# A long convolution and its expert layers: third stage one chunk later, last stage behind the first stage's visit, results stored whole

## The chip, the cores and the metric

The kernel runs on one core of one Trainium2 chip. A core has TensorE (matrix products into PSUM), VectorE (DVE), ScalarE (ACT), GpSimd (POOL) and SyncE (SP), which here issues every transfer between the chip's memory (HBM) and the core's SBUF. The engines run side by side, each through its own list of instructions in order, and wait for each other by semaphores. The metric is the time of one execution on the device in microseconds. All data are 32-bit floats.

## The reference

```python
def _attn_ref(x, v, pos_emb, w1, w2):          # x, v: (4, 12480, 128)
    h_mlp = np.maximum(pos_emb @ w1, 0.0) @ w2
    h_filt = h_mlp * np.exp(-0.01 * np.arange(S))[:, None]
    u = x * v
    Uf = np.fft.rfft(u, n=2 * S, axis=1)
    Hf = np.fft.rfft(h_filt, n=2 * S, axis=0)
    y = np.fft.irfft(Uf * Hf[None], n=2 * S, axis=1)[:, :S]
    return x * y

def _moe_ref(x, w_in, w_out):                  # x: (49920, 128), d_ff = 2048
    h = x @ w_in
    return (h * np.clip(h + 3.0, 0.0, 6.0) / 6.0) @ w_out
```

The result of the first function, reshaped to 49920 tokens, is the input of the second. So there is a causal convolution along the sequence, for every channel with its own filter, and then two dense layers with a gate between them.

## The kernel before, in words

**Convolution.** The Fourier transform along the sequence is split into products with small tables of sines and cosines. The 128 channels are taken in 4 groups of G = 32 and the 4 batches in 2 pairs, which makes NG = 8 groups of work, each with COLS = 128 columns. Two buffers z in SBUF hold the transforms of two groups at a time. For a group there are these stages:

- *First stage* (`first_stage`, L274): matmuls with `ctab` (L282) turn u = x * v into z; ScalarE copies the product from PSUM to z (L294). It is done in *visits* (`visit`, L457) of VISIT = 4 calls, for the group after the current one. The product x * v is made by GpSimd (`gate_next`, L453), which also sends for the next x and v (L442).
- *Spectra*, or second stage (`spectra`, L488; matmuls L301): K2 = 99 frequencies in NCHUNK = 25 chunks of CH = 4, each with a table `tab` of 256 KB that SP loads (`load_tab`, L471).
- *Products* (`products`, L503): ScalarE copies the spectra with their halves exchanged into the one bank `sw` (L499, L500); VectorE multiplies with the filter `h` (L520 to L523) into q, a, q2 and a2; GpSimd adds these (L527). SP loads the next `h` in two transfers of 128 KB (`load_h`, L484) into one of NH = 4 buffers.
- *Third stage* (`third_stage`, L536; matmuls L542): the same `tab` takes the sum `a` back; ScalarE copies it into z (L550). Then the table's buffer, one of NT = 7, is free and the next table is sent for.
- *Back* (`back`, L552): TensorE transposes four columns of z (L557) into a bank `ts`, and ScalarE copies them to `w` (L560). Sixteen columns fill a `w`, which is put on the list `pend`.
- *Fourth, or last, stage* (`fourth_stage`, L564): eight matmul records with `dtab` (L574) into two `ts` banks, a ScalarE copy to `o` (L584), a sum and a difference on VectorE (L586) give `y`. SP stores `y` row block by row block to the result tensors `yd`, in the order in which the expert layers will read, and the rows that fit no block of 32 to `ye` (L592, L595).

PSUM has eight banks: two for the spectra, one for `sw`, one for the third stage, and four `ts` banks that first stage, transposes and last stage share.

**The order of the work.** It is written out by hand (`manual_schedule`), and each engine does its share in that order. `period(g)` (L599) goes through the 25 chunks of a group. Chunk c does `products` of chunk c, `third_stage` of the chunk LAG - 1 = 2 before, `load_tab`, and `spectra` of chunk c + 1. Behind it come the transposes (`back`) of the group before, about 1.45 a chunk from chunk 2 on, each with up to three steps of decoding the expert weights (`weight`, L637; VectorE instructions L226 to L248, on up to group 6). After every fourth transpose comes one `fourth_stage` (from the eighth on; so it takes the `w` of one visit earlier) and then the visit of the next group. The `w` left over at the end of a group is taken in chunk 0 of the next group (L631). In group 0 nothing is transposed; in group 7 there is no visit.

**Turn-over.** `finish` (L653) does the last third stages, `last_turn` (L657) the 32 transposes and the last stages of group 7, with the first two loads of the expert layers among them.

**Expert layers** (class `Moe`, from L672): 98 tiles of 512 tokens, of which two hold the rows left over (`is_rest`). `load` (L709) brings x and the convolution's result `yt`, the latter in one transfer (L728), or for the two special tiles in transfers of one row's eighth (L722). `gate` (L733) multiplies them (L741), `turn` (L749) transposes and splits into high and low halves, `up` and `down` are the two layers, each in three matmuls per block (L768 to L770, L803 to L807), since a product is made of high and low parts. In tile t, `load(t + 2)` and `gate(t + 1)` are written out at steps 1 and 2 of 8.

Of the kernel before, what the change touches and what calls it, by code (L numbers as in the profile page):

```python
# [9 lines left out]
F32 = mybir.dt.float32  # L10
# [16 lines left out]
B, S, D = 4, 12480, 128  # L27
FO = 64
DFF = 2048
N1 = 64  # L30
N2 = 196
K2 = 99
NF = N1 * N2
R = (98, 97)
L = R[0] * N1
RH = R[0] // 2 + 1

G = 32
GB = 2
GY = 16  # L40
# [19 lines left out]

LAG = 3
NU = 2
# [3 lines left out]
GATES0 = (0, 2, 4, 8, 11, 14, 17, 20, 22)  # L66
NT = 7
NH = 4
# [91 lines left out]
def hyena_moe(ctx, tc, x, v, xt, pos_emb, w1, w2, w_in, w_out, c_tab, d_tab, f_tab, g_tab, win_d, ident_d, out):  # L160
# [4 lines left out]
    hd = [dram.tile([D // G // 2, P, K2, 2, G], F32, name=f"hd{h}") for h in range(2)]  # L165
    yd = [[dram.tile([NR, 4, 32, G // GH, N1, GH], F32, name=f"yd{b}_{k}") for k in range(2)] for b in range(B)]
    ye = dram.tile([len(REST), D // GH, N1, GH], F32, name="ye")
    wd = [dram.tile([2, P, DFF], F32, name=f"wd{i}") for i in range(2)]
# [8 lines left out]
    with tc.manual_schedule():  # L177
        conv = Conv(tc, nc, left, right, x, v, c_tab, d_tab, g_tab, ident, hd, yd, ye, weights)
        conv.filter(pos_emb, w1, w2, f_tab, win_d, ident_d)
        for g in range(NG):  # L180
            conv.period(g)
        conv.finish()
        left.close()
        moe = Moe(ctx, tc, nc, xt, wd, yd, ye, out)
        conv.last_turn(moe)
        right.close()
        moe.run()
# [64 lines left out]
class Conv:  # L252
    def __init__(self, tc, nc, left, right, x, v, c_tab, d_tab, g_tab, ident, hd, yd, ye, weights):
        self.tc, self.nc, self.left, self.right = tc, nc, left, right
        self.x, self.v, self.g_tab, self.ident, self.hd, self.yd = x, v, g_tab, ident, hd, yd
        self.c_tab, self.d_tab, self.weights, self.ye = c_tab, d_tab, weights, ye
        self.loaded, self.gated, self.n_loaded = [], [], 0
# [245 lines left out]
    def products(self, item):  # L503
# [4 lines left out]
        hs = self.hs.pop(0)  # L508
        a = self.pr.tile([P, CH, 2 * GB, G], F32, tag="a", name="pa")
        a2 = self.pr.tile([P, CH, 2 * GB, G], F32, tag="a2", name="pa2", bufs=2)  # L510
        q = self.pr.tile([P, CH, GB, G], F32, tag="q", name="pq", bufs=2)
        q2 = self.pr.tile([P, CH, GB, G], F32, tag="q2", name="pq2", bufs=2)
        uv = t.rearrange("p (k s g) -> p k s g", k=CH, g=G)[:, :kw]
# [38 lines left out]
    def back(self, g, col):  # L552

        nc = self.nc
        t = self.bank(("ts", "s2")[col // 4 % 2] if g == NG - 1 else "ts")
        for i in range(4):
            nc.tensor.transpose(t[:K2, i * 128 : (i + 1) * 128], self.z[g % 2][:, :, col + i], self.ident)  # L557
        if col % GY == 0:
            self.w = self.wp.tile([K2, GY, 128], F32, tag="w", name="w", bufs=3)
        nc.scalar.copy(self.w[:, col % GY : col % GY + 4, :].rearrange("p c m -> p (c m)"), t[:K2, :])  # L560
        if col % GY == GY - 4:
            self.pend.append((g, col + 4 - GY, self.w))

    def fourth_stage(self):  # L564
# [23 lines left out]
        k, b, d = self.place(g, piece)  # L588
        for h in range(2):
            e = ch // GH + h  # L590
            for i, p, q, r, n in PARTS:
                nc.sync.dma_start(self.yd[b][k][q, d // G, r : r + n, e], y[64 * h + p : 64 * h + p + n, i])  # L592
            for i, p, r in ((0, 49, 49), (1, 1, 97)):
                if r < R[k]:
                    nc.sync.dma_start(  # L595
                        self.ye[REST.index((b, k, r)), d // GH + e].unsqueeze(0), y[64 * h + p : 64 * h + p + 1, i]
                    )

    def period(self, g):  # L599
# [7 lines left out]
        for c in range(NCHUNK):  # L607
# [4 lines left out]
            while n < end:  # L612
# [4 lines left out]
                if n % VISIT == 0:  # L617
                    if n > VISIT:
                        self.fourth_stage()
                    if g + 1 < NG:  # L620
                        self.visit(g + 1, n // VISIT - 1)

    def chunk(self, g, c):
# [4 lines left out]
        if len(self.second) >= LAG:  # L628
            self.third_stage(self.second.pop(0))
            self.load_tab()  # L630
        if g > 1 and c == 0:  # L631
            self.fourth_stage()
        g, c = (g, c + 1) if c + 1 < NCHUNK else (g + 1, 0)
# [38 lines left out]
class Moe:  # L672
# [6 lines left out]

    def __init__(self, ctx, tc, nc, x, wd, yd, ye, out):  # L680
        self.ctx, self.tc, self.nc = ctx, tc, nc
        self.x, self.yd, self.ye, self.out = x, yd, ye, out
        P = 128
# [25 lines left out]
    def load(self, t):  # L709
# [4 lines left out]
        if self.is_rest(t):  # L714
            i = self.tiles[t]
            s = REST.index(i[0])
            for j in range(4):
                for m in range(len(i)):
                    a = self.ye[s + m, 4 * j : 4 * j + 4].rearrange("e (h r) c -> r h e c", r=32)
                    for h in range(2):  # L720
# [4 lines left out]
        else:  # L725
            b, k, q, n = self.tiles[t]
            a = self.yd[b][k][q].rearrange("q r e n c -> (q r) e n c")[:, :, n : n + self.NB, :]
            nc.sync.dma_start(  # L728
                y.rearrange("p (e m) -> p e m", e=4), a.rearrange("p e n c -> p e (n c)")
            )  # L730
        self.loaded[t] = xt, y

    def gate(self, t):  # L733
# [141 lines left out]
```

## Time and profile before

| What | Value |
|---|---|
| Median of 3 runs | 3256.47 us (3252.92 to 3272.07) |
| Profiled execution, device time | 3259.06 us |
| Its span, first to last instruction | 3257.3 us |
| TensorE, matmuls | 3156.4 us (97%) |
| ScalarE | 2356.5 us (72%) |
| VectorE | 2315.7 us (71%) |
| GpSimd | 2079.7 us (64%) |
| Bytes moved | 296.70 MB, mean 91 GB/s |

"Line engine op out<-in" names a group of instructions; "<-" behind a time names what ended the wait in front of it. PE is TensorE, PEld its weight loads, SPq the issuing of transfers on SP. A 32-bit matmul leaves two records, so eight records of L301 or L542 are the four matmuls of a chunk. The granted clock is TensorE's, as a share of full speed. The span is not the same everywhere: the filter's transform is made up to about 160 us, then come the eight groups, then a turn-over, and from about 1141 us the expert layers.

### The profile page before, as it was taken

How to read it: one execution, taken by the hardware profiler on the slowest of the kernel's cores; microseconds unless marked ns; L12 is line 12 of the kernel's file. 1: busy time of each engine (PE TensorE's matmuls, PEld its weight loads, DVE VectorE, ACT ScalarE, POOL GpSimd, SP SyncE). 2: the span in 40 equal slices, each digit the busy share in tenths (PEclk: the TensorE clock that was granted, in tenths of full speed). 3: DMA queues.
4: the chain of work that ended last, by engine and by line, in shares of the span. 5: the costliest groups of instructions: out<-in, count | busy, mean ns of one | idle time of the engine just before them, and what ended most of it. 6: DMA issues, size and time to landing. Idle time of an engine off the chain costs nothing.

```text
span 3257.3 us, 53858 instructions
## 1 busy us (share of the span) xinstructions
PE 3156.4 (97%) x20026; PEld 2667.5 (82%) x20026; DVE 2315.7 (71%) x2691; ACT 2356.5 (72%) x3039; POOL 2079.7 (64%) x1242
## 2 busy tenths in 40 slices
PE   9989899899899899999999999999999999999999
PEld 8988787787787588888888888888888888888887
DVE  4456676676656377777777777777777777777776
ACT  2356666666676577778877787778777877787777
POOL 1177767767767166666666666666666666666666
PEclk9999999999999999999999999999999999999999
DMA  6677777777765401011111111111111110111010
GB/s 232 198 202 193 206 194 196 206 200 193 203 173 168 141 30 39 30 36 39 39 39 34 36 39 39 33 36 40 39 30 39 39 39 30 39 39 39 30 39 23
DMA packets 236980, 296.70 MB, mean 91 GB/s; under 512 B 38727, under 2 KB 159854, under 8 KB 235694
## 3 DMA queue, kind: packets, MB, share of 16 engines
q1 hardware_dynamic: 236718, 293.26, 31.7%
q8 instruction: 158, 2.59, 0.3%
q14 instruction: 104, 0.85, 0.1%
HBM read 224.87 MB, written 68.29 MB: 90 GB/s over the span
## 4 chain that ended last, share of the span: by engine, by line
PE 66%; DMA 1%; SPq 0%; POOL 0%; ACT 0%; issue 0%; DVE 0%; DVEq 0%; ACTq 0%
PE acc L807 11%; PE acc L803 11%; PE acc L804 11%; PE ph L769 11%; PE ph L770 11%; PE ph L768 11%; DMA yd<-y 1%; PE ts L574 0%; PE ts L557 0%; SPq L592 0%; PE s L557 0%; DMA yt<-yd 0%; PE s L542 0%; PE s L301 0%; DMA ye<-y 0%; DMA tab<-in_g_tab 0%
## 5 line engine op out<-in xcount | busy, mean ns | idle before, releaser
L792 POOL TENSOR_TENSOR glo<-g,ghi 128x1024 fp32r<-128x1024 f32 x588 | 1404.3, 2396 | 775.4 <-ACT ghi L790 775.2
L780 DVE SCALAR_TENSOR_TENSOR g<-r,ph 128x1024 f32<-128x1024 f32 (+1 forms) x784 | 949.3, 1211 | 413.8 <-ACT r L778 413.6
L778 ACT ACTIVATE r<-ph,three 128x1024 f32<-128x1024 f32 (+1 forms) x784 | 871.4, 1112 | 277.6 <-PE ph L770 277.5
L790 ACT CAST ghi<-g 128x1024 fp32r<-128x1024 f32 (+1 forms) x784 | 811.1, 1035 | 5.4 <-DMA ye<-y 4.2
L768 PE MATMUL ph<-xhi,win_hi 128*128 128x512 f32 (+1 forms) x1568 | 609.1, 388 | 2.3 <-DVE y L586 2.3
L803 PE MATMUL acc<-ghi,wout_hi 128*128 128x512 f32 (+1 forms) x1568 | 608.6, 388 | 2.3 <-ACT ghi L790 2.3
L769 PE MATMUL ph<-xlo,win_hi 128*128 128x512 f32 (+1 forms) x1568 | 608.8, 388 | 0.0
L770 PE MATMUL ph<-xhi,win_lo 128*128 128x512 f32 (+1 forms) x1568 | 608.8, 388 | 0.0
L804 PE MATMUL acc<-ghi,wout_lo 128*128 128x512 f32 (+1 forms) x1568 | 608.6, 388 | 0.0
L807 PE MATMUL acc<-glo,wout_hi 128*128 128x512 f32 (+1 forms) x1568 | 481.8, 388 | 1.0 <-POOL glo L792 1.0
L527 POOL TENSOR_TENSOR pa<-pa,pq 128x256 f32<-128x256 f32 (+1 forms) x400 | 290.3, 732 | 247.4 <-DVE pa L521 220.8
L768 PEld LDWEIGHTS ph<-xhi,win_hi 128*128 128x128 f32 x1568 | 294.7, 188 | 64.2 <-issue 2.7
L803 PEld LDWEIGHTS acc<-ghi,wout_hi 128*128 128x128 f32 x1568 | 294.7, 188 | 63.4 <-ACT ghi L790 2.8
L807 PEld LDWEIGHTS acc<-glo,wout_hi 128*128 128x128 f32 x1568 | 294.0, 188 | 62.4 <-POOL glo L792 2.0
L770 PEld LDWEIGHTS ph<-xhi,win_lo 128*128 128x128 f32 x1568 | 294.6, 188 | 60.7
L804 PEld LDWEIGHTS acc<-ghi,wout_lo 128*128 128x128 f32 x1568 | 294.6, 188 | 60.6
L769 PEld LDWEIGHTS ph<-xlo,win_hi 128*128 128x128 f32 x1568 | 294.6, 188 | 60.5
L792 DVE TENSOR_TENSOR glo<-g,ghi 128x1024 fp32r<-128x1024 f32 x196 | 283.3, 1446 | 0.0
L520 DVE TENSOR_TENSOR pq<-s,h 128x256 f32<-128x256 f32 (+1 forms) x200 | 84.1, 420 | 280.0 <-POOL pa L527 124.3
L542 PE MATMUL s<-pa,tab 128*128 128x128 f32 x1694 | 242.3, 289 | 40.5 <-POOL pa L527 30.3
L542 PEld LDWEIGHTS s<-pa,tab 128*128 128x128 f32 x1694 | 212.4, 197 | 64.4 <-POOL pa L527 50.0
L741 DVE TENSOR_TENSOR xy<-xt,yt 128x512 f32<-128x512 f32 x96 | 260.3, 2711 | 0.0
(60 smaller groups left out, 3675.4 us busy)
## 6 DMA issues: line engine op xcount, KB each, us to landing
tab<-in_g_tab SPq DMA_DIRECT2D x192, 256.0 KB
h<-hd SPq DMA_DIRECT2D x384, 128.0 KB
xt<-in_xt SPq DMA_DIRECT2D x98, 256.0 KB
out<-o SPq DMA_DIRECT2D x97, 256.0 KB
xt<-in_x SPq DMA_DIRECT2D x64, 384.0 KB
vt<-in_v SPq DMA_DIRECT2D x64, 384.0 KB
yt<-yd SPq DMA_DIRECT2D x96, 256.0 KB
yd<-y SPq DMA_DIRECT2D x256, 64.0 KB
```

The lines of the kernel that those rows point to most:

```text
L527: nc.gpsimd.tensor_tensor(out=x, in0=x, in1=y, op=add)
L542: nc.tensor.matmul(t[:, i * 128 : (i + 1) * 128], tab[:, i, :], a[:, i].rearrange("p s g -> p (s g)"), start=(n == 0), stop=(n == len(term ...
L768: nc.tensor.matmul(ph[:, i, :ne], self.win_hi[:, sl], hi[:, :ne], start=True, stop=False)
L769: nc.tensor.matmul(ph[:, i, :ne], self.win_hi[:, sl], lo[:, :ne], start=False, stop=False)
L770: nc.tensor.matmul(ph[:, i, :ne], self.win_lo[:, sl], hi[:, :ne], start=False, stop=True)
L778: nc.scalar.activation(r[:, :, :ne], ph[:, :, :ne], AF.Relu, bias=self.three)
L780: nc.vector.scalar_tensor_tensor(out=g[:, :, :ne], in0=r[:, :, :ne], scalar=6.0, in1=ph[:, :, :ne], op0=ALU.min, op1=ALU.mult)
L790: nc.scalar.copy(ghi[:, :, :ne], g[:, :, :ne])
L792: e.tensor_tensor(out=glo[:, :, :ne], in0=g[:, :, :ne], in1=ghi[:, :, :ne].bitcast(F32), op=ALU.subtract)
L803: nc.tensor.matmul(a, self.wout_hi[:, f, :], ghi[:, i, :ne], start=(f == 0), stop=False)
L804: nc.tensor.matmul(a, self.wout_lo[:, f, :], ghi[:, i, :ne], start=False, stop=False)
L807: nc.tensor.matmul(a, self.wout_hi[:, f, :], glo[:, i, :ne], start=False, stop=(f == NFC - 1))
```

## The change

It has three parts.

1. *Lag and buffers.* LAG goes from 3 to 4, so a chunk's third stage comes three chunks behind its products and no longer two. The tables get eight buffers for seven, `a` four for three, and `a2`, `q` and `q2` three for two. `w` goes from three to two.
2. *Place of the last stage.* After every fourth transpose the visit comes first and `fourth_stage` right behind it, from the fourth transpose on, so it takes the `w` just filled. The call in chunk 0 is gone.
3. *Layout of the results.* `yd` takes the form of `y`, and one transfer of 512 KB stores a whole `y`. `ye` is gone. The expert layers' `load` now picks the rows out: one transfer for each of four channel groups where the block of 32 rows comes from one piece (two blocks of three), and two for each where it is made of 17 and 15 rows; the two special tiles take single rows from `yd` in as many transfers as before.

```diff
-LAG = 3
+LAG = 4
 NU = 2
 START = 2
 VISIT = 4
 GATES = (1, 4, 8, 11, 14, 17, 20, 22)
 GATES0 = (0, 2, 4, 8, 11, 14, 17, 20, 22)
-NT = 7
+NT = 8
 NH = 4
...
     dram = ctx.enter_context(tc.tile_pool(name="dram", bufs=1, space=DRAM))
     hd = [dram.tile([D // G // 2, P, K2, 2, G], F32, name=f"hd{h}") for h in range(2)]
-    yd = [[dram.tile([NR, 4, 32, G // GH, N1, GH], F32, name=f"yd{b}_{k}") for k in range(2)] for b in range(B)]
-    ye = dram.tile([len(REST), D // GH, N1, GH], F32, name="ye")
+    yd = [[dram.tile([D // G, G // GY, 2 * 64, 2, N1, GH], F32, name=f"yd{b}_{k}") for k in range(2)] for b in range(B)]
     wd = [dram.tile([2, P, DFF], F32, name=f"wd{i}") for i in range(2)]
     w_in = w_in.bitcast(I32).rearrange("p (q k c) -> q p k c", k=NW, c=2)
     w_out = w_out.bitcast(I32).rearrange("(q f p) (k c) -> q p f k c", f=NW // D, p=P, c=2)
...
         g, c, kw, t, tab = item
         sw = self.swapped(t, kw)
         hs = self.hs.pop(0)
-        a = self.pr.tile([P, CH, 2 * GB, G], F32, tag="a", name="pa")
-        a2 = self.pr.tile([P, CH, 2 * GB, G], F32, tag="a2", name="pa2", bufs=2)
-        q = self.pr.tile([P, CH, GB, G], F32, tag="q", name="pq", bufs=2)
-        q2 = self.pr.tile([P, CH, GB, G], F32, tag="q2", name="pq2", bufs=2)
+        a = self.pr.tile([P, CH, 2 * GB, G], F32, tag="a", name="pa", bufs=4)
+        a2 = self.pr.tile([P, CH, 2 * GB, G], F32, tag="a2", name="pa2")
+        q = self.pr.tile([P, CH, GB, G], F32, tag="q", name="pq")
+        q2 = self.pr.tile([P, CH, GB, G], F32, tag="q2", name="pq2")
         uv = t.rearrange("p (k s g) -> p k s g", k=CH, g=G)[:, :kw]
         sv = sw.rearrange("p (k s g) -> p k s g", k=CH, g=G)[:, :kw]
...
         for i in range(4):
             nc.tensor.transpose(t[:K2, i * 128 : (i + 1) * 128], self.z[g % 2][:, :, col + i], self.ident)
         if col % GY == 0:
-            self.w = self.wp.tile([K2, GY, 128], F32, tag="w", name="w", bufs=3)
+            self.w = self.wp.tile([K2, GY, 128], F32, tag="w", name="w")
         nc.scalar.copy(self.w[:, col % GY : col % GY + 4, :].rearrange("p c m -> p (c m)"), t[:K2, :])
         if col % GY == GY - 4:
             self.pend.append((g, col + 4 - GY, self.w))
...
             nc.vector.tensor_tensor(out=y[:, i], in0=same, in1=o, op=op)
         piece, ch = divmod(col, G)
         k, b, d = self.place(g, piece)
-        for h in range(2):
-            e = ch // GH + h
-            for i, p, q, r, n in PARTS:
-                nc.sync.dma_start(self.yd[b][k][q, d // G, r : r + n, e], y[64 * h + p : 64 * h + p + n, i])
-            for i, p, r in ((0, 49, 49), (1, 1, 97)):
-                if r < R[k]:
-                    nc.sync.dma_start(
-                        self.ye[REST.index((b, k, r)), d // GH + e].unsqueeze(0), y[64 * h + p : 64 * h + p + 1, i]
-                    )
+        nc.sync.dma_start(self.yd[b][k][d // G, ch // GY], y)
     def period(self, g):
...
                     self.weight(n)
                 n += 1
                 if n % VISIT == 0:
-                    if n > VISIT:
-                        self.fourth_stage()
                     if g + 1 < NG:
                         self.visit(g + 1, n // VISIT - 1)
+                    self.fourth_stage()
     def chunk(self, g, c):
...
         if len(self.second) >= LAG:
             self.third_stage(self.second.pop(0))
             self.load_tab()
-        if g > 1 and c == 0:
-            self.fourth_stage()
         g, c = (g, c + 1) if c + 1 < NCHUNK else (g + 1, 0)
         if g < NG:
             self.first.append(self.spectra(g, c))
...
         y = self.io.tile([128, 512], F32, tag="y", name="yt", bufs=3)
         nc.sync.dma_start(xt, self.x[t])
         if self.is_rest(t):
-            i = self.tiles[t]
-            s = REST.index(i[0])
-            for j in range(4):
-                for m in range(len(i)):
-                    a = self.ye[s + m, 4 * j : 4 * j + 4].rearrange("e (h r) c -> r h e c", r=32)
+            for m, (b, k, r) in enumerate(self.tiles[t]):
+                i, p = (0, r) if r < RH else (1, R[0] - r)
+                for j in range(4):
+                    a = self.parts(b, k, j, i, p, p + 1)[0].rearrange("e (h r) c -> r h e c", r=32)
                     for h in range(2):
                         cols = slice(64 * m + 32 * h, 64 * m + 32 * h + 32)
                         nc.sync.dma_start(
...
                         )
         else:
             b, k, q, n = self.tiles[t]
-            a = self.yd[b][k][q].rearrange("q r e n c -> (q r) e n c")[:, :, n : n + self.NB, :]
-            nc.sync.dma_start(
-                y.rearrange("p (e m) -> p e m", e=4), a.rearrange("p e n c -> p e (n c)")
-            )
+            for i, p, block, r, m in PARTS:
+                for j in range(4 if block == q else 0):
+                    a = self.parts(b, k, j, i, p, p + m)[:, :, n : n + self.NB, :]
+                    nc.sync.dma_start(
+                        y[32 * j + r : 32 * j + r + m, :].rearrange("r (e m) -> r e m", e=4),
+                        a.rearrange("r e n c -> r e (n c)"),
+                    )
         self.loaded[t] = xt, y
+
+    def parts(self, b, k, j, i, p0, p1):
+
+        return self.yd[b][k][j].rearrange("f (e p) i n c -> i p (f e) n c", p=64)[i, p0:p1]
     def gate(self, t):
```

The rest of the diff takes `ye` out of the lists of arguments.

More of the change, by code (lines that the diff above doesn't have):

```diff
@@ L177, in hyena_moe @@
     with tc.manual_schedule():
-        conv = Conv(tc, nc, left, right, x, v, c_tab, d_tab, g_tab, ident, hd, yd, ye, weights)
+        conv = Conv(tc, nc, left, right, x, v, c_tab, d_tab, g_tab, ident, hd, yd, weights)
         conv.filter(pos_emb, w1, w2, f_tab, win_d, ident_d)
@@ L183, in hyena_moe @@
         left.close()
-        moe = Moe(ctx, tc, nc, xt, wd, yd, ye, out)
+        moe = Moe(ctx, tc, nc, xt, wd, yd, out)
         conv.last_turn(moe)
@@ L252, with __init__ @@
 class Conv:
-    def __init__(self, tc, nc, left, right, x, v, c_tab, d_tab, g_tab, ident, hd, yd, ye, weights):
+    def __init__(self, tc, nc, left, right, x, v, c_tab, d_tab, g_tab, ident, hd, yd, weights):
         self.tc, self.nc, self.left, self.right = tc, nc, left, right
         self.x, self.v, self.g_tab, self.ident, self.hd, self.yd = x, v, g_tab, ident, hd, yd
-        self.c_tab, self.d_tab, self.weights, self.ye = c_tab, d_tab, weights, ye
+        self.c_tab, self.d_tab, self.weights = c_tab, d_tab, weights
         self.loaded, self.gated, self.n_loaded = [], [], 0
@@ L678, with __init__ @@
     NB = 16
-    def __init__(self, ctx, tc, nc, x, wd, yd, ye, out):
+    def __init__(self, ctx, tc, nc, x, wd, yd, out):
         self.ctx, self.tc, self.nc = ctx, tc, nc
-        self.x, self.yd, self.ye, self.out = x, yd, ye, out
+        self.x, self.yd, self.out = x, yd, out
         P = 128
```

## The prediction

> **What bounds the kernel now.** I read the page first, for the engine that is never free, then the same busy times by stage, with the stages cut where a group's first second-stage matmul starts.
>
> ```profile
> span 3257.3 us, 53858 instructions
> PE 3156.4 (97%) x20026; PEld 2667.5 (82%) x20026; DVE 2315.7 (71%) x2691; ACT 2356.5 (72%) x3039; POOL 2079.7 (64%) x1242
> ```
>
> In the next rows the columns are the window, its length, busy PE, PEld, DVE, ACT and POOL, the granted clock, the DMA engines' share and GB/s: group 0, groups 1 to 6, group 7, the turn-over, the expert layers.
>
> ```profile
> 160.00:252.00 92.00, 82.68 (x999) 78.38 (x1000) 47.25 (x98) 54.92 (x104) 68.73 (x68) 1.00 0.79 199
> 252.00:978.20 726.20, 662.60 (x6601) 581.58 (x6600) 478.54 (x870) 474.92 (x896) 515.21 (x496) 0.97 0.74 196
> 978.20:1064.00 85.80, 81.46 (x567) 68.80 (x566) 55.14 (x110) 59.15 (x110) 63.26 (x71) 1.00 0.57 167
> 1064.00:1141.00 77.00, 65.03 (x287) 43.43 (x287) 27.55 (x40) 38.59 (x62) 13.91 (x11) 0.91 0.44 138
> 1141.00:3257.30 2116.30, 2111.97 (x9362) 1750.13 (x9360) 1631.92 (x1362) 1677.66 (x1754) 1397.03 (x586) 1.00 0.12 36
> ```
>
> The expert layers are TensorE without a hole (2112.0 of 2116.3): nothing to win there. In groups 1 to 6 TensorE is idle for 726.2 - 662.6 = 63.6 us, and the clock 0.97 takes more. Group 0 has 9.3 us idle, group 7 4.3, the turn-over 12.0. TensorE's waits in groups 1 to 6 (total, times, longest) say where the 63.6 come from:
>
> ```profile
> PE s L542 <- POOL pa L527: 22.4, 38, 1.6
> PE s L301 <- DMA tab<-in_g_tab: 19.1, 11, 3.1
> PE ts L557 <- DVE y L586: 15.3, 5, 3.5
> PE s L301 <- DVE pa L521: 2.6, 1, 2.6
> PE s L542 <- ACT sw L499: 2.3, 1, 2.3
> ```
>
> The clock hangs on these waits: in the windows view, the 3.6 us that hold a table wait of 1.72 us run at 1.00, the next 3.4 us at 0.50, whatever is in them.
>
> ```profile
> 642.00:645.60 3.60, 1.88 (x15) 1.72 (x14) 2.26 (x6) 1.77 (x4) 3.03 (x4) 1.00 1.10 261
> 645.60:649.00 3.40, 3.40 (x17) 3.40 (x17) 3.26 (x7) 2.60 (x5) 2.37 (x3) 0.50 1.10 258
> ```
>
> A mean of 0.97 over 726.2 us is a loss of 3%, about 20 us: some twelve such stretches, each costing half of 3.4. So a floor for groups 1 to 6 is 726 - 64 - 20 = 642 us, 107 a group; with the other stages' idle time the convolution could give back about 100 us.
>
> **The stores leave SP's queue.** TensorE's timeline around that table wait, then SP's:
>
> ```profile
> 624.21 1.16 PE L542 MATMUL s<-pa,tab 128*128 128x128 f32 x8 [0.86 <-POOL pa L527]
> ...
> 641.35 1.06 PE L542 MATMUL s<-pa,tab 128*128 128x128 f32 x8
> 644.13 1.13 PE L301 MATMUL s<-z,tab 128*128 128x128 f32 x8 [1.72 <-DMA tab<-in_g_tab]
> ```
>
> ```profile
> 628.73 1.53 SPq L592 DMA_DIRECT2D yd<-y  x4
> 630.31 0.25 SPq L595 DMA_DIRECT2D ye<-y  x1
> 630.60 1.46 SPq L592 DMA_DIRECT2D yd<-y  x4
> 632.10 0.86 SPq L595 DMA_DIRECT2D ye<-y  x1
> ...
> 638.99 0.54 SPq L471 DMA_DIRECT2D tab<-in_g_tab  x1
> ```
>
> Counting loads back from the stalled L301 (seven buffers), its table went into the buffer that the L542 at 624.21 released by 625.4; SP issued the load only at 638.99, 13.6 us later, and 4.6 us ahead of need. In between, one result tile alone took 1.53 + 0.25 + 1.46 + 0.86 = 4.1 us of SP. The change puts one issue there. Not seen before; nearest is the table load's 0.54, so 3.6 us saved eight times a group, 29 us of SP's 121. Table and filter loads move forward by about a result tile's 3.6 us, more where two tiles lie ahead, against a longest wait of 3.1. Of the 19.1 us I take 15; the bounds are 19.1 and 0 (if transfers, not issuing, are late).
>
> What the store adds: SP stops on it until y is complete, and the next chunk's h and tab loads queue behind. It is issued after y in both kernels, and y comes one visit (2.9 us, below) later, less than the 3.6 saved: nothing, at worst as much as the gain. It moves the whole tile, 512 KB for about 390, so 1 MB a group more. What the DMA engines do in group 4:
>
> ```profile
> q1 hardware_dynamic: 16701, 24.22, 75.5%
> yd<-y SPq DMA_DIRECT2D x16, 34.0 KB
> ```
>
> 75.5% of 120.7 us is 91 us for 24.2 MB; 25.2 MB take 95 at that rate, still under 107.
>
> The Trainium skill, "DMA: Bandwidth & Descriptors", section "Why a DMA increments its semaphore by 16 and not by 1", lets a transfer use the largest count up to 16 that divides its outer size: the 34.0 KB stores (17 rows) would sit on one DMA engine, the new 128-row store on all. By it that engine is freed as well, and the term would be nearer 19 than 15; no view here tells the engines apart.
>
> **The last stage behind the visit.** DVE and TensorE at one of the five waits for y:
>
> ```profile
> 721.13 1.43 DVE L242 SCALAR_TENSOR_TENSOR dec<-dec 128x256 f32<-128x256 int32 x1
> 722.49 1.27 DVE L586 TENSOR_TENSOR y<-ts,o 128x512 f32<-128x512 f32 x2
> ```
>
> ```profile
> 716.40 1.94 PE L574 MATMUL ts<-w,dtab 99*64 99x512 f32 x8
> 718.17 2.91 PE L282 MATMUL ts<-ctab,u 97*64 97x99 f32 x64
> 723.82 1.14 PE L557 MATMUL ts<-ident,z 128*99 128x128 f32 x4 [2.73 <-DVE y L586]
> ```
>
> L586 stands behind weight decoding on DVE and holds a ts bank; the visit uses up the others, and the next transpose stops. Afterwards the visit runs first, decoding ends under it, and after L574 come third stage and spectra (1.06 + 1.13 us above), which need no ts bank. I take 14 of 15.3; bounds 15.3 and 0. The moved o copy and y put the next chunk's products about 1.3 us (L586) later; the third stage's extra chunk, over 2 us, covers that.
>
> L574 now reads a w just copied; the 2.91 us of L282 cover the copy. Group 7 has no visit. The nearest rows are the turn-over's last, where L574 directly follows the transposes:
>
> ```profile
> 1117.61 1.07 PE L574 MATMUL ts<-w,dtab 99*64 99x512 f32 x2 [1.82 <-ACT w L560]
> 1119.07 1.93 PE L574 MATMUL ts<-w,dtab 99*64 99x512 f32 x6 [0.39 <-ACT w L560]
> ```
>
> The upper bound is 8 x 2.2 = 18 us; ScalarE was behind with expert work there, and the first quarter of L574 needs only older columns. The lower is 0. I take the 0.39 row and half as much again, 0.6 x 8 = +5. The call at chunk 0 merely moves its 1.9 us. Two w buffers do: one filling, one waiting.
>
> **The third stage a chunk later.** GpSimd's adds in group 4 (count, busy, mean ns):
>
> ```profile
> L527 POOL TENSOR_TENSOR pa<-pa,pq 128x256 f32<-128x256 f32 x48 | 35.3, 745 | 29.2 <-DVE pa L521 27.4
> L527 POOL TENSOR_TENSOR pa<-pa,pa 128x512 f32<-128x512 f32 x24 | 30.9, 1289 | 1.9
> ```
>
> A chunk costs GpSimd 2 x 0.745 + 1.289 = 2.8 us, more than the 2.2 us a chunk without transposes costs TensorE: at a group's start TensorE catches up. Over the group GpSimd is busy 515 of 726, so one chunk of lead, at least 2.2 us, covers each single wait (longest 1.6). But the last stage no longer fills chunk 0 (1.9 us), so I take 16 of 22.4; bounds 22.4 and 0. The third product buffer lets DVE run on, and eight tables keep the prefetch as deep as seven did: with the two one-off waits (2.6 and 2.3) 4 us, bounds 5 and 0. Group 0 gives 2 of 9.3, group 7 3 of 4.3.
>
> The lag has a price. A group's last chunk, 24, now goes through the third stage in chunk 2 of the next group, right ahead of that group's first transpose, which reads all of z; before, a whole chunk lay between. ScalarE's copy to z stands behind the next chunk's two sw copies. The nearest rows are the turn-over's first transpose, directly behind its z copy, and one sw copy's group:
>
> ```profile
> 1074.69 1.18 PE L557 MATMUL ts<-ident,z 128*99 128x128 f32 x4 [0.57 <-ACT z L550]
> ```
>
> ```profile
> L500 ACT ACTIVATE sw<-s 64x512 f32<-64x512 f32 (+1 forms) x200 | 113.1, 566 | 6.4
> ```
>
> So a new wait of 0.57 us with ScalarE free, 0.57 + 2 x 0.57 = 1.7 with both copies ahead, in seven groups: 4 to 12 us. I take 8; the lower end is 0, if the spectra between cover it.
>
> **The clock.** Where the waits go, so do the half-speed stretches: 16 of 20 us, as the GpSimd waits, mostly under 1 us, hardly cause any. Bounds 20 and 0.
> The Trainium skill, "TensorE: Matmul & The Clock Gate", section "Why this matters for your kernels", ties the drop to gaps of over about 3 us. By that, most of these stretches have another cause and this term would be near 5, the sum -50; the 1.72 us wait above, with 0.50 right behind it, speaks against it.
>
> **Expert layers and turn-over.** A tile's results come in 4 or 8 loads instead of one. SP's and DVE's rows for one tile:
>
> ```profile
> 2007.69 0.53 SPq L728 DMA_DIRECT2D yt<-yd  x1
> ```
>
> ```profile
> 2038.02 2.78 DVE L741 TENSOR_TENSOR xy<-xt,yt 128x512 f32<-128x512 f32 x1
> ```
>
> Loads go out 30 us before use, so 7 x 0.53 = 3.7 us more issuing is hidden: cost 0. Without that cover, 32 tiles with 8 loads and 64 with 4 would cost 32 x 3.7 + 64 x 1.6 = 220 us. In the turn-over 12 us idle partly hang on the many stores; I take 4, bounds 8 and 0.
>
> **The sum:** -15 - 14 + 5 - 16 - 4 - 2 - 3 + 8 - 16 - 4 = -61 against the profiled execution's 3259.06 us (2 us around the span): 3198. The median shown is 3256.47, 2.6 lower: 3195. All best ends together (19.1 + 15.3 + 22.4 + 5 + 20 + 8, plus 8 of groups 0 and 7, nothing added) give -98, 3158.
>
> **Rivals.** *Transfers, not issuing* (16%): in the table wait above the DMA engines ran full at 261 GB/s, so the table may be late although issued early; then the table term (15), half the clock's (8) and 6 of GpSimd's stay: -61 + 29 = -32, 3224. For it: the 4.6 us from issue to use were not enough. Against: the group's mean is 0.74. The Trainium skill, "DMA: Bandwidth & Descriptors", section "Issuing engines are not separate DMA queues", holds issuing time to be usually small beside the transfer, which is this rival; the 13.6 us above speak against it.
> *Slower: L574 waits for ScalarE* (8%): if the queue of ScalarE is over 2.9 us behind when the transposes end, the visit covers nothing, and the 48 calls of groups 1 to 6 each pay the 2.2 us of the turn-over: +106 on -61, 3301. For it: ScalarE's own waits for DVE stand in that queue. Against: it is busy 475 of 726 us.
> *Nothing moves* (8%): the freed waits return as others at the same place, GpSimd and DVE pacing TensorE at the old 121 us a group, and only the turn-over's 4 us are won: 3252. Against: neither is over 71% busy there.
> The forecast keeps 68%, within 3162 to 3222.
>
> **Numbers.** Under 1% is what measuring cannot tell from no change, 33 us here. Faster by more: the forecast and half of the transfer rival, 0.75; within: the other half and nothing-moves, 0.16; slower 0.09. The range runs from 3162 to 3238: it leaves out slower, nothing-moves and a few beyond.
>
> **What would show it.** Right: a group near 109 to 111 us, table and y waits under 5 us in groups 1 to 6, clock 0.99 or more there, one SP issue of about half a microsecond per result tile, small L574 waits in group 7 alone, an L557 wait for z of about a microsecond once a group, expert layers still 2116. Wrong: table waits left with SP idle (transfers), L574 waiting for w in every group (slower rival), or the clock still 0.97 with the long waits gone.

## The result, and the profile after

The changed kernel takes 3208.74 us (median, 3207.41 to 3210.08) against 3256.64 us for the kernel before beside it: ratio 0.9844, 95% interval 0.9812 to 0.9876. The forecast was 3195 us, so the direction and most of the way were right and 14 us were missing. The profiled span went from 3257.3 to 3207.9 us, 49.4 us less.

The page of the changed kernel:

```profile
span 3207.9 us, 53636 instructions
...
PE 3142.8 (98%) x20026; PEld 2650.7 (83%) x20026; DVE 2308.7 (72%) x2691; ACT 2346.3 (73%) x3039; POOL 2078.8 (65%) x1242
```

Its stages, cut as before (window, length, busy PE, PEld, DVE, ACT, POOL, granted clock, DMA share, GB/s): groups 1 to 6, group 7, turn-over, expert layers.

```profile
251.10:934.00 682.90, 647.10 (x6617) 564.20 (x6616) 474.23 (x871) 466.50 (x899) 515.21 (x496) 1.00 0.76 218
934.00:1026.30 92.30, 87.72 (x568) 70.03 (x566) 56.09 (x112) 59.07 (x110) 63.18 (x71) 1.00 0.53 168
1026.30:1092.00 65.70, 61.79 (x287) 43.36 (x287) 24.40 (x36) 38.88 (x62) 11.89 (x11) 0.92 0.46 168
1092.00:3207.90 2115.90, 2111.65 (x9360) 1749.87 (x9359) 1631.75 (x1364) 1676.96 (x1754) 1398.73 (x586) 1.00 0.12 36
```

Groups 1 to 6 give 726.2 - 682.9 = 43.3 us: TensorE's idle time falls from 63.6 to 682.9 - 647.1 = 35.8, and its busy time by 662.6 - 647.1 = 15.5 for the same work, because the clock is 1.00 and no longer 0.97. Group 7 is longer (85.8 to 92.3), the turn-over shorter (77.0 to 65.7), group 0 shorter by 0.9, the expert layers the same within 0.4. Together -43.3 + 6.5 - 11.3 - 0.9 - 0.4 = -49.4.

What TensorE waits for in groups 1 to 6 of the changed kernel (total, times, longest):

```profile
PE s L541 <- ACT z L549: 25.2, 35, 1.3
PE ts L556 <- ACT z L549: 7.1, 6, 1.3
PE s L300 <- DVE pa L520: 2.5, 5, 0.5
```

L541, L556, L300 and L549 are the third stage, the transposes, the spectra and the copy to z, one line higher than before. The waits for tables, for y and for GpSimd are gone. In their place stands mainly one cause, ScalarE's copy to z. The transposes' part was in the forecast. The third stage's 25.2 us were not: they are the missing gain. The timeline of a group's start shows how they come about (start, length, engine, line, operation; in brackets the idle time ahead and what ended it):

```profile
594.78 1.26 POOL L526 TENSOR_TENSOR pa<-pa,pq 128x192 f32<-128x192 f32 x2 [1.64 <-DVE pa L520]
...
594.85 0.38 SPq L588 DMA_DIRECT2D yd<-y  x1
...
595.48 0.56 ACT L498 COPY sw<-s 64x512 f32<-64x512 f32 x1 [1.41 <-DVE pa L522]
596.07 0.57 ACT L499 ACTIVATE sw<-s 64x512 f32<-64x512 f32 x1
...
596.56 0.58 ACT L549 COPY z<-s 128x512 f32<-128x512 f32 x1
596.73 0.42 DVE L519 TENSOR_TENSOR pq<-s,h 128x256 f32<-128x256 f32 x1 [1.36 <-POOL pa L526]
...
597.29 1.13 PE L541 MATMUL s<-pa,tab 128*128 128x128 f32 x8 [1.05 <-ACT z L549]
...
598.00 0.68 DVE L522 TENSOR_TENSOR pa<-sw,h 128x512 f32<-128x512 f32 x1
...
598.79 0.56 ACT L498 COPY sw<-s 64x512 f32<-64x512 f32 x1 [1.64 <-DVE pa L522]
```

The row of L588 is the new store: one issue of 0.38 us where 4.1 us stood. The others are a ring. The copies to sw (L498, L499: 1.16 us) wait until VectorE's L522 has read the one bank sw; VectorE's products (L519 to L522, 596.73 to 598.68: 1.95 us) begin when the copies are done. (The row of L519 names GpSimd's add, but that ended at 594.78 + 1.26 = 596.04; the copies end at 596.07 + 0.57 = 596.64, 0.09 us before the products start.) So a round takes 598.79 - 595.48 = 3.31 us, and the two engines, neither full, take turns. TensorE needs about 2.2 us for such a chunk (1.06 + 1.13). The copy to z stands in ScalarE's queue behind the copies to sw, and the one bank of the third stage is free for the next L541 only after it. As soon as a few chunks without transposes follow one another, TensorE runs at the ring's pace.

### The profile page after: what moved, and what is told of

It is laid out like the page before. It is cut to its first block, busy times and chain, and to the rows that moved or that the text cites. A ratio compares the mean times of both kernels' runs of the same rounds, so it can differ in the third digit from the quotient of the medians.

```text
span 3207.9 us, 53636 instructions
## 1 busy us (share of the span) xinstructions
PE 3142.8 (98%) x20026; PEld 2650.7 (83%) x20026; DVE 2308.7 (72%) x2691; ACT 2346.3 (73%) x3039; POOL 2078.8 (65%) x1242
## 3 DMA queue, kind: packets, MB, share of 16 engines
q1 hardware_dynamic: 231726, 301.25, 31.7%
## 4 chain that ended last, share of the span: by engine, by line
PE 68%; ACT 0%; DVE 0%; POOL 0%; DMA 0%; issue 0%; ACTq 0%; DVEq 0%
PE acc L801 11%; PE acc L798 11%; PE acc L797 11%; PE ph L763 11%; PE ph L764 11%; PE ph L762 11%; PE ts L573 1%; PE ts L556 1%; PE s L541 0%; PE s L556 0%; PE s L300 0%; DMA yd<-y 0%; POOL glo L786 0%; ACT z L549 0%; DVE y L585 0%
## 5 line engine op out<-in xcount | busy, mean ns | idle before, releaser
L541 PEld LDWEIGHTS s<-pa,tab 128*128 128x128 f32 x1694 | 207.2, 193 | 84.8 <-POOL pa L526 50.1
L541 PE MATMUL s<-pa,tab 128*128 128x128 f32 x1694 | 237.0, 285 | 36.5 <-ACT z L549 35.2
L526 POOL TENSOR_TENSOR pa<-pa,pa 128x512 f32<-128x512 f32 (+1 forms) x186 | 236.8, 1273 | 14.6
```

The costliest lines, as they stand in the source:

```text
L526: nc.gpsimd.tensor_tensor(out=x, in0=x, in1=y, op=add)
L541: nc.tensor.matmul(t[:, i * 128 : (i + 1) * 128], tab[:, i, :], a[:, i].rearrange("p s g -> p (s g)"), start=(n == 0), stop=(n == len(term ...
```

## The experiments

The change has three parts, and all combinations were run. They are told first with the stores changed, then with the stores as they were, then the tests of single causes. A line "TensorE's waits" is that view from 160 to 1141 us, that is the convolution and the turn-over. Ratios are to the kernel before on the same chip, in brackets the 95% interval; microseconds between kernels of different chips are differences of ratios times 3260.

**Stores alone.** The kernel before with the new layout, stores and loads; lag, buffers and the last stage's place as before.

```diff
-                nc.sync.dma_start(self.yd[b][k][q, d // G, r : r + n, e], y[64 * h + p : 64 * h + p + n, i])
...
+        nc.sync.dma_start(self.yd[b][k][d // G, ch // GY], y)
```

> The kernel before with the new layout of the results alone (one store of 512 KB per result tile, loads in 4 or 8 pieces). Theory A, issuing on SP is what made the tables late: TensorE's table waits in groups 1 to 6 (19.1 us before) fall under 4, half-speed stretches behind them go, the y waits (15.3) and GpSimd waits (22.4) stay, the turn-over gives its 11.7 us: 3215 to 3228 us. Theory B, the transfers themselves were late: the table waits stay above 12 us and the time is 3240 to 3250, the turn-over's gain alone.

3213.26 us, ratio 0.9858 (0.9841 to 0.9875). TensorE's waits:

```profile
PE s L541 <- POOL pa L526: 31.3, 51, 2.3
PE s L541 <- ACT sw L498: 9.2, 4, 2.3
PE s L541 <- ACT z L549: 7.6, 16, 1.5
PE ts L556 <- DVE y L585: 4.4, 10, 0.9
```

The stores alone are worth as much as the whole change within the intervals; the time is 2 us below Theory A's range. The table waits (19.3 us of the kernel before in this view) are gone, as forecast. The waits for y, however, which Theory A kept, fell too, from 16.0 to 4.4, though the last stage stayed where it was and VectorE's weight decoding with it. VectorE was not earlier. Here is the same transpose, the 29th in group 4, that waited 2.73 us until 723.82 in the kernel before (it was ready at 721.09), and the y that stands beside it:

```profile
703.02 0.94 PE L556 MATMUL ts<-ident,z 128*99 128x128 f32 x4
```

```profile
704.60 1.28 DVE L585 TENSOR_TENSOR y<-ts,o 128x512 f32<-128x512 f32 x2
```

In both kernels y starts 13.1 us after the same products (709.35 to 722.49 before, 691.45 to 704.60 here), but here the transpose runs before y has even started and waits for nothing. The two programs differ in the bank: in the kernel before as built, this transpose has the ts bank that y is still read from, in each of groups 1 to 5; with the new stores the same code was given another of the four. So these 11.6 us came neither through SP's queue nor from the place of the last stage, where the forecast had booked them, and they are luck of the build. What they and the clock behind them make of the whole gain was not measured by itself.

**Stores and lag, without the new place.** The changed kernel with the last stage at its old place (two w buffers).

```diff
+                    if n > VISIT:
+                        self.fourth_stage()
                     if g + 1 < NG:
                         self.visit(g + 1, n // VISIT - 1)
-                    self.fourth_stage()
...
+        if g > 1 and c == 0:
+            self.fourth_stage()
```

> The changed kernel with the last stage at its old place (one visit late, ahead of the visit, and in chunk 0), still with two w buffers. Theory A, the new place is a loss by itself: group 7 falls from 92.3 back to 85.9 us because L574's copy is old again, the last stage fills chunk 0 again, and nothing is lost in groups 1 to 6, where stores alone already left only 4 us of waits for y: 3193 to 3203 us. Theory B, the new place is what lets the long lag work (y waits come back as prefetch grows): 3208 or more.

3191.20 us, ratio 0.9780 (0.9764 to 0.9797): faster than the whole change by (0.9844 - 0.9780) x 3260 = 21 us, so Theory A, 2 us below its range. TensorE's waits:

```profile
PE s L541 <- ACT z L549: 16.0, 34, 1.3
PE ts L556 <- ACT z L549: 9.0, 8, 1.3
PE ts L556 <- DVE y L585: 7.9, 11, 1.0
```

and of the changed kernel in this view, with the same L556 row:

```profile
PE s L541 <- ACT z L549: 35.2, 50, 1.3
```

The y waits come back with 7.9 us, but the third stage's waits for z are 16.0 where the changed kernel has 35.2. The reading is that the last stage in chunk 0, about 1.9 us a group, had given the ring time, and that behind a visit it gives none, as TensorE is slow enough there anyway; no run moved that call alone. Of the 18.8 us between the two profiled spans, 682.9 - 673.1 = 9.8 lie in groups 1 to 6 and 92.3 - 84.4 = 7.9 in group 7.

**Stores and place, without the lag.** The changed kernel with LAG, tables and products as before (`w` in two buffers).

```diff
-LAG = 4
+LAG = 3
...
-NT = 8
+NT = 7
```

> The changed kernel with LAG 3, seven tables and the old product buffers, so stores and order alone. Theory A, the longer lag gave nothing net, the GpSimd waits only came back as waits for the copy to z: TensorE waits some 25 us for GpSimd in groups 1 to 6 where the changed kernel waits 25 for z, and the time is within 6 us of the changed kernel's 3208.7. Theory B, as predicted, the lag is worth its 16 + 4 - 8 us: 3220 or more.

3231.09 us, ratio 0.9911 (0.9894 to 0.9928). TensorE's waits:

```profile
PE s L541 <- POOL pa L526: 43.9, 57, 2.3
PE s L541 <- ACT z L549: 14.6, 26, 1.2
```

This is Theory B. On the same chip as the stores alone: the new place costs 3231.09 - 3213.26 = 17.8 us here too. GpSimd's waits grow from 31.3 to 43.9 and z's from 7.6 to 14.6, which fits the lost cover in chunk 0. The lag is worth (0.9858 - 0.9780) x 3260 = 25 us without the new place and (0.9911 - 0.9844) x 3260 = 22 with it.

**Place alone, lag alone, both, with the old stores.** The same edits on the kernel before.

> The kernel before with the new place of the last stage alone (behind the visit; no call in chunk 0; two w buffers). Theory A, the parts add up: the y waits (15.3 us) and the half-speed stretches behind them (5 x 1.7) go, group 7 loses 6.6, table waits stay at about 19: 3237 to 3243 us. Theory B, while SP is late one wait only gives way to the next: table and filter waits grow by what the y waits lose, 3250 to 3262.

> The kernel before with the longer lag and the added buffers alone (w in two buffers). Theory A, while the stores keep the tables late the lag is worth nothing: GpSimd waits (22.4 us in groups 1 to 6) go, table waits grow by as much or more, 3250 to 3262. Theory B, the parts add up and the lag is worth the 22 us that it gave beside the new stores: 3236 to 3243.

> The changed kernel with the old stores and loads, so lag, buffers and order alone. Theory A, the stores are what frees SP: table waits of 15 us or more and a clock of 0.98 or less in groups 1 to 6, the turn-over as before, 3232 to 3245 us. Theory B, a table has more slack with eight buffers and a later third stage: table waits under 8 us, 3222 to 3230.

Place alone 3267.99 us, ratio 1.0021 (1.0011 to 1.0031); lag alone 3257.28, 0.9988 (0.9979 to 0.9997); both 3261.92, 1.0004 (0.9993 to 1.0015). The largest of TensorE's waits, for place alone:

```profile
PE s L301 <- DMA tab<-in_g_tab: 30.7, 21, 3.1
PE s L542 <- POOL pa L527: 30.5, 43, 1.8
PE s L542 <- ACT z L550: 16.0, 27, 1.5
```

for lag alone:

```profile
PE s L301 <- DMA tab<-in_g_tab: 28.3, 18, 3.9
PE s L542 <- ACT z L550: 16.0, 34, 1.3
...
PE s L301 <- DVE pa L521: 13.7, 11, 2.9
```

and for both:

```profile
PE s L301 <- DMA tab<-in_g_tab: 35.1, 20, 3.4
PE s L542 <- ACT z L550: 31.3, 48, 1.3
```

Each edit removes the wait that it was made for: y with the new place, nearly all of GpSimd's 30.3 with the lag. The time hardly moves, because other waits grow in return: for tables from 19.3 to 30.7, 28.3 and 35.1, for z at L542 from 7.6 to 16.0, 16.0 and 31.3, and with the lag alone for VectorE's `pa` from 4.2 to 13.7. VectorE itself waits 18.2 us there for filter loads from SP's queue, where it was 5.2. So with SP late a good part of what is won elsewhere is lost again at loads that are not there, and another part at the copy to z. The parts are not a sum: the lag is worth 4 us with the old stores and 25 with the new. Lag alone came out as Theory A had it; place alone lies 6 us above its Theory B, and for both together the two ranges, 3222 to 3245, were missed by 17 us.

**One store or eight.** The changed kernel, each result stored in eight transfers of 16 partitions: the same bytes and rows, seven more issues per tile.

```diff
-        nc.sync.dma_start(self.yd[b][k][d // G, ch // GY], y)
+        for p in range(0, 128, 16):
+            nc.sync.dma_start(self.yd[b][k][d // G, ch // GY, p : p + 16], y[p : p + 16])
```

> The changed kernel with each result stored in eight transfers of 16 partitions, the same bytes. SP then issues eight stores for a result tile, as the kernel before did beside its one to four small ones. Theory A, issuing is what counted: SP loses about 8 x 0.35 = 2.8 us a tile, some table waits return, 3212 to 3230. Theory B, one or few DMA engines were overloaded by the stores of 17 rows: nothing changes, 3205 to 3211.

**Eight stores, one of them of 17 partitions.** As that kernel, but the partitions are cut 16, 17, 15 and five times 16.

```diff
-        for p in range(0, 128, 16):
-            nc.sync.dma_start(self.yd[b][k][d // G, ch // GY, p : p + 16], y[p : p + 16])
+        for p, n in ((0, 16), (16, 17), (33, 15), (48, 16), (64, 16), (80, 16), (96, 16), (112, 16)):
+            nc.sync.dma_start(self.yd[b][k][d // G, ch // GY, p : p + n], y[p : p + n])
```

> The same eight transfers with the second of 17 and the third of 15 partitions, so 17 rows of 4 KB, 70 KB, in one transfer, as much as the two stores of 34 KB had before. Theory A (issuing): the same time as with eight transfers of 16, within 3 us. Theory B, a transfer of 17 rows sits on one DMA engine: table waits return here and not there, 8 us or more slower than with 16.

3234.82 us, ratio 0.9915 (0.9901 to 0.9930), and 3267.68 us, ratio 1.0026 (1.0015 to 1.0036). The tables in TensorE's waits, of the eight equal stores:

```profile
PE s L300 <- DMA tab<-in_g_tab: 16.9, 9, 4.2
```

and with one of 17:

```profile
PE s L300 <- DMA tab<-in_g_tab: 38.9, 20, 4.2
```

Seven more issues a tile bring the table waits back and cost (0.9915 - 0.9844) x 3260 = 23 us; the time is 5 us above Theory A's range. The rows of SP's timeline in group 4 add up to 88.6 us of issuing in the kernel before, 63.9 in the changed one and 89.3 with eight stores: issuing counts. (The eight also bring 3% more packets, 238894 for 231726, so it need not be all.) One cut moved by one partition, with neither an issue nor a byte more, costs another 33 us on the same chip, as its Theory B had it. The two kernels differ in nothing but that 17- and 15-partition pair. The Trainium skill, "DMA: Bandwidth & Descriptors", section "Why a DMA increments its semaphore by 16 and not by 1", gives a transfer the largest count of DMA engines up to 16 that divides its outer size: one engine for 17, 15 for 15, 16 for 16. The run agrees with it in sign; no view told the engines apart.

**The stores before, 17 rows as 16 and 1.** The kernel before, each of its two 17-row stores per tile cut in two.

```diff
-                nc.sync.dma_start(self.yd[b][k][q, d // G, r : r + n, e], y[64 * h + p : 64 * h + p + n, i])
+                for s, m in ((0, 16), (16, 1)) if n == 17 else ((0, n),):
+                    rows = y[64 * h + p + s : 64 * h + p + s + m, i]
+                    nc.sync.dma_start(self.yd[b][k][q, d // G, r + s : r + s + m, e], rows)
```

> The kernel before with each store of 17 rows made in two, 16 rows and 1 row: the same bytes, two more issues on SP for every result tile (0.6 us). Theory A, issuing alone made the tables late: slower, by 8 x 0.6 us in each of six groups where SP has no slack, 3262 to 3290. Theory B, the 17 rows on one DMA engine were the larger part (33 of the 59 us that eight stores cost the changed kernel): faster than before in spite of the issues, table waits under 12 us in groups 1 to 6, 3225 to 3248.

3288.06 us, ratio 1.0089 (1.0074 to 1.0104). TensorE's waits for tables:

```profile
PE s L301 <- DMA tab<-in_g_tab: 45.1, 23, 4.1
```

With no 17-row transfer left and two more issues a tile the table waits rise from 19.3 to 45.1, and the time lies in Theory A's range, although the waits for y fall from 16.0 to 8.9 (this program, too, was built with another order of the ts banks). In the kernel before, two more issues (each for a store of a single row, whose own price was not measured) cost more than the long transfers did. Both causes are real, then. How its 19 us of table waits divide between them stays open, since a store with neither more issues nor 17 rows is the new layout itself.

**A second bank for the swapped spectra.** If the ring is the cause, a second sw bank must open it. It is taken from the four ts banks.

```diff
-    BANKS = {"s2": 2, "sw": 1, "s3": 1, "ts": 4}
+    BANKS = {"s2": 2, "sw": 2, "s3": 1, "ts": 3}
```

> The changed kernel with two PSUM banks for sw and three instead of four for ts. Theory A, at a group's start ScalarE and VectorE take turns on the one sw bank, 3.3 us a chunk, and the copy to z stands in that queue: the waits for the copy to z (32 us in groups 1 to 6) fall under 16, and if three ts banks cost nothing the time is 3185 to 3198. Theory B, it is the single bank of the third stage: these waits stay above 25 us, time 3205 to 3215. If three ts banks are too few, new waits of L281 or L556 for ScalarE or VectorE show it.

3169.55 us, ratio 0.9715 (0.9700 to 0.9729), (0.9844 - 0.9715) x 3260 = 42 us below the changed kernel and 15 below Theory A's range. TensorE's waits:

```profile
PE s L541 <- ACT z L549: 6.4, 17, 1.2
PE s L300 <- DVE pa L520: 6.0, 7, 1.1
PE s L300 <- DMA tab<-in_g_tab: 2.1, 5, 0.7
```

and ScalarE at a group's start:

```profile
576.59 0.56 ACT L498 COPY sw<-s 64x512 f32<-64x512 f32 x1 [0.30 <-PE s L300]
...
578.49 0.56 ACT L498 COPY sw<-s 64x512 f32<-64x512 f32 x1 [0.23 <-PE s L300]
```

ScalarE now waits for TensorE, no longer for VectorE; a round takes 1.90 us and not 3.31. Third stage and transposes together waited 35.2 + 9.0 us for z, and now 6.4 + 0.6. The ring is shown. A group takes (900.5 - 243.3) / 6 = 109.5 us for 682.9 / 6 = 113.8.

**The old place with the second bank.** The kernel with stores and lag, last stage at its old place, banks as above.

> Two banks for sw and the last stage at its old place everywhere, so stores, lag and the second sw bank. If the new place was a loss only through group 7 and the sw queue at a group's start, both now relieved, this ties with the version above, 3160 to 3168. If three ts banks are too few when the last stage stands ahead of the visit, waits for y return on the first-stage or transpose matmuls, 3172 to 3200.

3236.29 us, ratio 0.9925 (0.9911 to 0.9939): the second bank, worth 42 us with the new place, costs 47 with the old one. Both ranges (3160 to 3168, 3172 to 3200) were too low. TensorE's waits:

```profile
PE ts L281 <- DVE y L585: 26.4, 6, 4.5
PE ts L556 <- DVE y L585: 14.1, 5, 2.8
```

Here is the mechanism that the forecast gave for the y waits, at full size: y stands behind weight decoding, holds its ts bank, and with three banks the visit itself (L281) and the next transposes stop. (At the longest such wait decoding runs until 400.27, y from 400.19 to 401.46, and the visit goes on at 401.52.) So, in these programs as built, the new place is worth (0.9925 - 0.9715) x 3260 = 68 us where three banks are to do, and costs 21 where there are four. It is what frees the bank for sw.

**Group 7 with an older w.** The kernel with two sw banks; in group 7, where no visit covers the copy to w, the last stage comes two transposes later.

```diff
                     if g + 1 < NG:
                         self.visit(g + 1, n // VISIT - 1)
+                        self.fourth_stage()
+                if g + 1 == NG and n % VISIT == 2:
                     self.fourth_stage()
```

> The changed kernel with two banks for sw and, in group 7 alone, the last stage two transposes later, so that it reads a w copied before. If group 7's loss is L574's wait for a fresh copy, its L574 time falls from 18.3 to 13.2 us and the whole to 3162 to 3166; if it only moves elsewhere, 3168 or more.

3164.14 us, ratio 0.9702 (0.9689 to 0.9716), 5.4 us under the other kernel's 3169.55 by the medians, 4.2 by the ratios; the intervals overlap. The stage itself shows it. Weight loads of L573 in group 7 of the changed kernel, count, lengths and what ended the idle time ahead of them:

```profile
L573 PEld LDWEIGHTS ts<-w,dtab x56: 132/136/137, 951.6 to 1020.1; 99*64 99x64 f32 x56
its engine sat idle before it (us, times) until:
  ACT w L559: 5.4, 7
  issue: 4.0, 14
```

and of this kernel:

```profile
L573 PEld LDWEIGHTS ts<-w,dtab x56: 132/136/137, 921.9 to 981.1; 99*64 99x64 f32 x56
its engine sat idle before it (us, times) until:
  issue: 4.0, 14
```

The wait for w is gone; in the kernel with the two banks alone it was 3.9 us, 7 times. There these matmuls are busy for 18.74 us of group 7 and here for 13.56, and group 7 is 80.7 us for 85.9. This is the fastest version of all, 46 us under the changed kernel ((0.9844 - 0.9702) x 3260).

## Why the prediction was right, and where it was off

The bottleneck was read rightly: the expert layers had nothing to give (2115.9 for 2116.3), the time lay in TensorE's waits in groups 1 to 6, and SP's queue was a main cause of them. Of the signs set down for being right, one did not come: a group takes 113.8 us and not 109 to 111. The terms, one after the other, in groups 1 to 6 unless said:

- *Stores* (table waits, -15). Right: -19.1, the upper bound. That it was issuing and not transfers alone is borne out by the eight equal stores, which bring SP's issuing and the table waits back. One reading of the forecast is off: the table load was not out 4.6 us ahead of need; these are its 4.6 us from the end of the issue, 639.53, to the start of the delayed L301, which was ready 1.72 us earlier, so 2.9 us ahead. The sentence on the one engine for 17 rows was closer than the forecast made of it: a single such transfer a tile cost 33 us in the changed kernel. The transfer rival, table waits left over, did not come. The eight loads per tile in the expert layers cost nothing, as said.
- *Last stage behind the visit* (y waits, -14). The number came, -15.3, but the step failed. The forecast put these waits down to VectorE's queue and the visit's banks, and the runs bear that mechanism out; but it took the place of the last stage for the only cure, and did not ask which bank the waiting transpose is given. The program built with the new stores gives it another, and so the stores alone took 11.6 of 16.0. What is left for the new place is 4 to 8 us of short waits (longest 1.0), and for them it gives away the cover in chunk 0 and the covered w in group 7: 18 to 21 us lost beside the new stores. The sentence "the last stage no longer fills chunk 0" had the loss in sight and sized it within GpSimd's term; it should have been charged to this one.
- *w just copied* (+5 in group 7, none in groups 1 to 6). Right: 5.4 us over seven of eight calls, and no wait for w among the rows of groups 1 to 6, nor among those of TensorE's weight loads, so the slower rival did not come.
- *Lag* (GpSimd -16, buffers -4). GpSimd's 22.4 us and the two one-off waits are gone, all of it. But the forecast asked only whether GpSimd had a chunk of lead, and not what is late next: the ring of the one sw bank, 25.2 us at L541. The rows for it stood in the profile before: ScalarE's sw copies (0.57 us each) and VectorE's share were known, and "a chunk without transposes costs TensorE 2.2 us" was compared with GpSimd's 2.8 alone. Compared with copies and products one after the other, 3.3 us, it would have shown the next bound. In group 7, too, z's 3.2 + 1.3 us took the place of GpSimd's 4, so the 3 us won there fell away; group 0 won 0.9 of 2.
- *Transposes wait for z* (+8). Right: 9.0 in all, 1.3 us once a group.
- *Clock* (-16). Right: TensorE's busy time fell by 15.5 and the mean is 1.00. The twelve half-speed stretches are gone; five of them stood behind the waits for y.
- *Turn-over* (-4). Undersized: 11.3 us, beyond the bound of 8. Its idle time fell from 12.0 to 3.9 and its busy time by 3.2. It comes from the stores, for which VectorE waited 18.9 + 3.5 us there before it could write the next y; with the new stores that wait is gone. From the end of group 7 to the end of the span the kernel with the stores alone takes 3213.6 - 1032.5 = 2181.1 us, the changed one 3207.9 - 1026.3 = 2181.6, the one before 3257.3 - 1064.0 = 2193.3. The row for it was there, 12.0 us idle, and the forecast took a third of it. The clock gave little, 0.92 for 0.91.

Idle time in groups 1 to 6 adds up: -19.1 - 15.3 - 22.4 - 2.6 - 2.3 + 25.2 + 7.1 + 2.5 = -26.9, for 27.8 measured. Against the forecast, groups 1 to 6 fell short by some 15 us (the ring's 25, less the 12 that table, y and GpSimd gave beyond their terms, and small ones) and group 7 by 3.5, with a seventh of the transposes' 8 us counted to group 7; the turn-over gave 7 back. So that only 14 us were missing is in part luck, and so is the number of the y waits.

## What to carry to other kernels

When a change takes a wait away, work out the pace of every ring that is then left, above all of two engines that fill and empty one buffer in turn: their times add up, even if each is half idle. Settle a late issuing queue first, since until then a part of every other repair is lost again at its loads (the lag was worth 4 us before the stores were changed and 25 after). Where stages share buffers, find out which buffer the built program gave to the instruction that waits: a change elsewhere can move it, and the gain is then not that change's own. And judge a move by the cover that it takes from its old place and by the buffers that it needs: here the same move cost 21 us with four banks and was worth 68 with three.

## What was not expected of the hardware

A store cut at 17 partitions in place of 16 cost 33 us over 64 tiles, about half a microsecond each, without a byte or an issue more; TensorE's clock went down with it, as the windows of groups 1 to 6 show, of the kernel with eight equal stores and then of the one with a cut of 17:

```profile
251.50:955.20 703.70, 655.95 (x6616) 572.42 (x6615) 474.84 (x871) 467.72 (x899) 515.49 (x496) 0.99 0.82 211
```

```profile
250.40:984.50 734.10, 669.11 (x6617) 585.37 (x6616) 474.94 (x871) 468.97 (x899) 515.47 (x496) 0.96 0.78 202
```

Of the 30.4 us between these two rows 669.1 - 656.0 = 13.2 are busy time of the same matmuls, that is clock. (The profiled execution of the second is 8 us above its median, so the rows show it somewhat large.)

The clock does not follow the idle time as a whole, and the length of one wait does not settle it either. The changed kernel is idle for 35.8 us of 682.9 in groups 1 to 6, in waits of at most 1.3 us, and its clock is 1.00 there; the kernel before, with waits of up to 3.5 us, had 0.97. But of two waits of 2.30 us at the same line and for the same copy, in the run with stores and place and without the lag, the one that ended at 267.25 had a stretch at half speed behind it and the one that ended at 385.54 had none:

```profile
268.00:271.40 3.40, 3.40 (x18) 3.40 (x17) 1.85 (x4) 0.67 (x2) 3.24 (x5) 0.50 1.06 255
...
386.00:389.40 3.40, 3.40 (x35) 3.28 (x35) 1.95 (x4) 1.73 (x4) 3.32 (x5) 1.00 1.05 277
```

And in the changed kernel's turn-over, where no wait is longer than 1.2 us, two of them (1.16 and 0.77 us) stand within 3.1 us, and behind them the clock is at half for 10.2 us:

```profile
1034.90:1045.10 10.20, 8.86 (x40) 8.30 (x40) 0.00 (x0) 4.08 (x8) 0.80 (x1) 0.50 1.00 411
```

The Trainium skill, "TensorE: Matmul & The Clock Gate", section "Why this matters for your kernels", puts the bound at gaps of about 3 us; the 1.72 us wait of the kernel before had a stretch at 0.50 behind it, so here the measurement decides: half speed came behind shorter waits too. Which of them cost it is not resolved.
